# Seven block products back from FF in every other step, eight in the others, and the gate read from the accumulator banks

## The chip, the cores and the metric

The kernel runs on one core of a Trainium2 chip. The time is device microseconds of one execution: 3052.83 us as the median of three runs (3049.15 to 3056.44). The profiled execution took 3051.49 us, of which 3049.7 us is the span from its first to its last instruction. The engines are named as in the profile: PE (matrix products; PEld its weight loads), DVE, ACT and POOL (elementwise work), SP (issues the transfers). PSUM is the memory of eight banks that PE accumulates into; DVE and ACT read it, POOL does not.

## The reference

```python
X = np.fft.rfft(x, axis=1)                       # x: 8 x 3008 x 256
Yr = Xr @ w_r - Xi @ w_i + b_r                   # 256 x 256 weights
Yi = Xr @ w_i + Xi @ w_r + b_i
Yr = np.sign(Yr) * np.maximum(np.abs(Yr) - 0.01, 0.0)     # the same for Yi
y = np.fft.irfft(Yr + 1j * Yi, n=3008, axis=1)   # 24064 tokens of 256
h = y @ w_in                                     # 256 x 2048
g = h * np.clip(h + 3.0, 0.0, 6.0) / 6.0
return g @ w_out                                 # 2048 x 256
```

Nearly all the work is in the last three lines, which are called FF below.

## The kernel before, in words

**FF in steps.** The tokens are cut into 47 chunks of 512. The 2048 hidden features are cut into 4 quarters of 512. A step is one chunk and one quarter, so there are 188 of them (`quads`). Both matrix products of a step are made as a 2 x 2 block product by Winograd's scheme, with seven block products where the plain scheme needs eight. On the way into FF (`up_1` to `up_7`) they are accumulated in two PSUM banks, `px` and `py`: `up_1` starts `px`, ACT copies it into `py` (L966), `up_2` adds to `py`, and so on, until four blocks of h (128 features x 512 tokens each, `hs[i][:, 0..3]`) are read out. Every block product is done as three passes of fp32r matmuls over two halves, since each operand is a high and a low part: six matmuls of 256 columns (L943).

**The gate and the operands for the way back.** Block 0 is gated straight from `py`: ACT makes relu(h + 3) (L972), DVE takes the minimum with 6 and multiplies by h (L973). Blocks 1, 2 and 3 are first brought to SBUF (L990 and L1000 on DVE, L995 on ACT) and gated there in the next step, two blocks at once and then one (L1006 on ACT, L1007 on DVE). Then Winograd's sums of the gated blocks are formed on POOL: T1 and T3 in one subtraction (L1016), T2 (L1038) and nT4 (L1039). Each of b11, b22, b21, T1, T3, T2, nT4 is split into a high part by ACT (`split`, L134) and a low part, the rest, by a subtraction (L135). The subtraction is on DVE for all but b11, where it is on POOL. They go two at a time (1024 columns), b11 alone (512).

**The way back** (`down`): seven block products, accumulated over the four quarters in the banks `z0` to `z3`, with weights that are loaded from DRAM for every step (`load_weights`, L1047, 256 KB for one product). After a chunk's last quarter the four banks are combined and sent out (`finish`, L1075, L1085).

**The order.** Iteration i of the main loop holds `up` of step i, the elementwise work of step i-1 and `down` of step i-2. The code calls their parts in an order that is written out by hand, and into eight slots of an iteration it lays the pieces of the Fourier part of the next sequences (`fill`): that part makes the tokens (`segment`, `stage1`, `middle`, with their own matmuls into the two `side` banks) and, by `prepare`, the seven operands `yb` of the way in, with sums (L913) and low parts on POOL (L135). Engines work through their queues in order, and a scheduler may swap calls that lie close together. The program begins with some 127 us in which the first sequence is transformed and the weights are split; the steps follow.

In the profile L134 and L135 are the two lines of `split`, whatever calls it; the names of the tiles tell which: g (operands of the way back), yb (of the way in), X, z, xs (Fourier part).

Of the kernel before, what the change touches and what calls it, by code (L numbers as in the profile page):

```python
# [25 lines left out]
P = 128  # L26
# [75 lines left out]
def spectral_ffn(ctx: ExitStack, tc: tile.TileContext, x, w_r, w_i, bias, w_in, w_out, f47, f64, g64, g64u, sgn, out):  # L102
# [7 lines left out]
    depth = {"g2": 3, "yb": 7, "wo": 7, "raw": 2, "h": 2, "r": 3, "ot": 2, "bt": 2, "f64": 2}  # L110

    def space(shape, dt, name, tag=None):
        tag = tag or name
        return sb.tile(shape, dt, name=name, tag=tag, bufs=depth.get(tag, 1))
# [57 lines left out]
    wout_d = [dram.tile([7, P, 2, 2, P], F32, name=f"w_out{q}") for q in range(nf // 2)]  # L172
# [22 lines left out]
    class Band:  # L195

        def __init__(self, into, f, tags, home):
            self.into, self.f, self.home = into, f, home
            src = w_in if into else w_out
# [21 lines left out]
        def rest(self):  # L221
# [8 lines left out]
            s = self.sums = self.st.bitcast(F32).rearrange("p (n c) w -> p n (c w)", n=8)[:, :4]  # L230
            for to, p, q, op in (
# [8 lines left out]
        def opened(self):  # L240
            if not hasattr(self, "forms"):
                if self.into:
                    self.forms = [t[:, self.f] for t in win_s]
                else:
                    self.pair = space([P, 7, 2, P], F32R, "wt", self.home)
                    self.forms = [self.pair[:, :, n] for n in range(2)]
            return self.forms

        def upper(self):
            nc.scalar.copy(out=self.opened()[0][:, :3], in_=self.value[:, 1:])  # L250

        def sums_hi(self):
            nc.scalar.copy(out=self.opened()[0][:, 3:], in_=self.sums)

        def sums_lo(self):
            for part, src in ((slice(0, 3), self.value[:, 1:]), (slice(3, 7), self.sums)):
                hi, lo = (t[:, part] for t in self.forms)
                nc.vector.tensor_tensor(out=lo, in0=src, in1=hi.bitcast(F32), op=ALU.subtract)
            if not self.into:
                q, half = divmod(self.f, 2)  # L260
                nc.sync.dma_start(out=wout_d[q][:, :, half].rearrange("m p w c -> p m w c"), in_=self.pair.bitcast(F32))
# [446 lines left out]
    def middle(b):  # L708
# [11 lines left out]
        def s2(g):  # L720
# [16 lines left out]
            xi = space([P, 2, P], F32, "xi")  # L737
# [70 lines left out]
    def segment(b, k):  # L808
# [35 lines left out]
        def odd_part(ps, n):  # L844
            odd = space([P, 2 * R47], F32, "odd", "wo" if begins else "xi")[:, :n]
# [83 lines left out]
    SLOT = {"b11": 0, "b12": 1, "b22": 2, "b21": 3}  # L929
    DOWN = (("b21", 2, "z0", 1), ("b11", 1, "z0", 0), ("b22", 3, "z2", 0), ("T1", 5, "z2", 1))  # L930
    DOWN += (("T3", 7, "z1", 0), ("T2", 6, "z1", 1), ("nT4", 4, "z3", 0))
# [3 lines left out]
    def behind_start(ins, first):  # L935
        tc.add_manual_dep(ins.ins, first.ins.name, after, reason="bank cleared")

    def passes(to, weight, moving, start, stop=True, first=None, later=False):
# [3 lines left out]
        for n, (a, b) in enumerate(todo):  # L942
# [3 lines left out]
            if n == 0:  # L946
                begin_ = ins
                if first is not None:
                    behind_start(ins, first)
        return begin_  # L950
# [17 lines left out]
    def up_2(i):  # L968
        py = keep.pop((i, "y"))
        block(i, 2, py, False)  # L970
        r = space([P, T], F32, "p1")
        nc.scalar.activation(out=r, in_=py, func=AF.Relu, bias=3.0, scale=1.0)  # L972
        nc.vector.scalar_tensor_tensor(out=hs[i][:, 0], in0=r, scalar=6.0, in1=py, op0=ALU.min, op1=ALU.mult)  # L973
# [28 lines left out]
    def gate(i, at):  # L1002

        h = hs[i][:, at]
        r = space([P, *h.shape[1:]], F32, "r")
        nc.scalar.activation(out=r, in_=h, func=AF.Relu, bias=3.0, scale=1.0)  # L1006
        nc.vector.scalar_tensor_tensor(out=h, in0=r, scalar=6.0, in1=h, op0=ALU.min, op1=ALU.mult)  # L1007

    def gate_2(i):
        gate(i, slice(2, 4))  # L1010

    def gate_1(i):
        gate(i, 1)
        h = hs[i]
        t = keep[i, "T13"] = space([P, 2, T], F32, "r")
# [287 lines left out]
```

## Time and profile before

| | before |
|---|---|
| median of 3 runs | 3052.83 us |
| the profiled execution | 3051.49 us, span 3049.7 us |
| busy share of the span | PE 86%, PEld 82%, DVE 84%, ACT 67%, POOL 76% |
| mean granted PE clock | 0.959 of full speed |
| matmuls | 19,887, of which 15,792 in FF |
| loads of the weights of the way back | 1,316 of 256 KB |

A duration in the profile runs from the start to the end of an instruction, so it holds whatever the instruction waited for once it had begun. The ends of matmuls are modelled, and neighbours overlap; the distance between their starts is the pace. "Idle before" is time in which an engine had nothing running, put down to what ended it.

### The profile page before, as it was taken

What the parts mean: (1) busy time and instruction counts of PE and PEld (TensorE: products, weight loads), DVE (VectorE), ACT (ScalarE), POOL (GpSimd) and SP (SyncE); (2) the same over time, 40 slices, a digit from 0 to 9 for tenths busy, and PEclk for the clock granted to TensorE, in tenths of its full rate; (3) what the DMA queues carried; (4) which work ended last, traced back from release to release, by engine and by line L of the source; (5) the groups of instructions that cost most, each with busy time, mean ns of one, the idle gap of its engine ahead of it and who ended that gap; (6) DMA issues with size and microseconds to landing.
All of it is one profiled execution on the core that took longest, in us unless ns stands there. A gap on an engine that the chain in (4) does not pass through costs nothing.

```text
span 3049.7 us, 55092 instructions
## 1 busy us (share of the span) xinstructions
PE 2637.1 (86%) x19887; PEld 2500.2 (82%) x19887; DVE 2570.9 (84%) x3011; ACT 2033.8 (67%) x3480; POOL 2330.0 (76%) x1490
## 2 busy tenths in 40 slices
PE   9688888888888888888898888888798898898888
PEld 6578888878887888888888888888788888888887
DVE  6778888987897889988897888888788998878787
ACT  5566766766666666666666766667576766666665
POOL 3286787887787877788876887788876776788887
PEclk9899999999999999999999999999999999999999
DMA  7765665665655656556565655666556555555554
GB/s 264 245 183 173 199 198 167 195 200 164 183 166 183 187 168 189 175 179 191 166 185 173 184 183 178 183 190 194 165 177 183 174 175 168 172 162 163 153 156 153
DMA packets 343913, 552.66 MB, mean 181 GB/s; under 512 B 37471, under 2 KB 130007, under 8 KB 343639
## 3 DMA queue, kind: packets, MB, share of 16 engines
q1 hardware_dynamic: 343639, 549.14, 58.9%
q8 instruction: 156, 2.56, 0.4%
q14 instruction: 118, 0.97, 0.1%
HBM read 444.66 MB, written 82.31 MB: 173 GB/s over the span
## 4 chain that ended last, share of the span: by engine, by line
POOL 28%; DVE 22%; PE 19%; issue 12%; ACT 11%; DMA 3%; SPq 0%; POOLq 0%; DVEq 0%; ACTq 0%
POOL r L1016 8%; PE z L943 6%; DVE g L135 6%; POOL yb L135 5%; POOL r L1039 4%; DVE h L1007 4%; PE py L943 4%; PE side L141 4%; POOL r L1038 4%; ACT g L134 4%; PE px L943 4%; POOL g L135 3%; DVE tc L767 2%; POOL T L913 2%; DVE ot L1075 1%
## 5 line engine op out<-in xcount | busy, mean ns | idle before, releaser
L943 PE MATMUL z<-g,wo 128*128 128x256 f32 x7896 | 1136.1, 288 | 6.4 <-DVE g L135 2.3
L943 PEld LDWEIGHTS z<-g,wo 128*128 128x128 f32 x7896 | 1043.7, 196 | 16.3 <-DVE g L135 3.2
L135 DVE TENSOR_TENSOR g<-r,g 128x1024 fp32r<-128x1024 f32 x376 | 560.3, 1490 | 155.1 <-ACT g L134 147.8
L134 ACT CAST g<-r 128x1024 fp32r<-128x1024 f32 x376 | 394.4, 1049 | 426.8 <-POOL r L1016 191.4
L943 PE MATMUL px<-yb,w_in_hi 128*128 128x256 f32 x3008 | 581.7, 286 | 1.4 <-POOL yb L135 1.4
L943 PE MATMUL py<-yb,w_in_lo 128*128 128x256 f32 x1128 | 353.6, 313 | 217.2 <-ACT py L966 102.7
L1016 POOL TENSOR_TENSOR r<-h 128x1024 f32<-128x1024 f32 x188 | 487.4, 2592 | 49.3 <-DVE h L1007 46.4
L135 DVE TENSOR_TENSOR g<-h,g 128x1024 fp32r<-128x1024 f32 x188 | 428.6, 2280 | 87.2 <-ACT g L134 86.1
L1007 DVE SCALAR_TENSOR_TENSOR h<-r,h 128x1024 f32<-128x1024 f32 x376 | 486.9, 1302 | 14.1 <-ACT r L1006 12.8
L943 PE MATMUL px<-yb,w_in_lo 128*128 128x256 f32 x1504 | 443.3, 295 | 46.5 <-ACT h L995 31.5
L943 PEld LDWEIGHTS px<-yb,w_in_hi 128*128 128x128 f32 x3008 | 474.6, 194 | 5.1 <-POOL yb L135 1.8
L135 POOL TENSOR_TENSOR g<-h,g 128x512 fp32r<-128x512 f32 x188 | 308.8, 1642 | 180.4 <-ACT g L134 167.5
L943 PEld LDWEIGHTS py<-yb,w_in_lo 128*128 128x128 f32 x1128 | 218.9, 194 | 270.4 <-ACT py L966 123.8
L943 PE MATMUL py<-yb,w_in_hi 128*128 128x256 f32 x2256 | 439.2, 287 | 0.0
L943 PEld LDWEIGHTS py<-yb,w_in_hi 128*128 128x128 f32 x2256 | 358.5, 195 | 1.9 <-issue 0.5
L1039 POOL TENSOR_TENSOR r<-h,r 128x512 f32<-128x512 f32 x188 | 342.4, 1821 | 11.2
L1006 ACT ACTIVATE r<-h 128x1024 f32<-128x1024 f32 x376 | 318.3, 847 | 40.8 <-DVE h L990 36.0
L943 PEld LDWEIGHTS px<-yb,w_in_lo 128*128 128x128 f32 x1504 | 292.7, 195 | 64.2 <-ACT h L995 39.3
L1038 POOL TENSOR_TENSOR r<-h,r 128x512 f32<-128x512 f32 x188 | 327.8, 1744 | 9.7
L134 ACT CAST g<-h 128x512 fp32r<-128x512 f32 x376 | 313.8, 835 | 26.6 <-PE z L943 15.0
L977 ACT COPY u<-px 128x512 f32<-128x512 f32 x376 | 221.2, 588 | 84.1 <-PE px L943 80.4
L135 POOL TENSOR_TENSOR yb<-raw,yb 128x256 fp32r<-128x256 f32 x138 | 160.4, 1163 | 114.0 <-ACT yb L134 113.7
(205 smaller groups left out, 4605.2 us busy)
## 6 DMA issues: line engine op xcount, KB each, us to landing
wo<-w_out SPq DMA_DIRECT2D x1316, 256.0 KB, 3.2
xin<-in_x SPq DMA_DIRECT2D x48, 512.0 KB, 4.3
bt<-scr SPq DMA_DIRECT2D x96, 256.0 KB, 3.3
scr<-pt SPq DMA_DIRECT2D x96, 256.0 KB, 2.9
out<-ot SPq DMA_DIRECT2D x94, 256.0 KB, 3.2
scr<-a SPq DMA_DIRECT2D x96, 240.0 KB, 3.1
qt<-scr SPq DMA_DIRECT2D x96, 240.0 KB, 4.2
zt<-tc SPq DMA_DIRECT2D x336, 64.0 KB, 2.0
```

What stands on the lines that cost most here:

```text
L134: nc.scalar.copy(out=hi, in_=src)
L135: (on or nc.vector).tensor_tensor(out=lo, in0=src, in1=hi.bitcast(F32), op=ALU.subtract)
L141: nc.tensor.matmul(out=ps, lhsT=a, rhs=b, start=start and n == 0, stop=stop and n == len(todo) - 1, skip_group_check=more,)
L767: nc.vector.scalar_tensor_tensor(out=t, in0=t, scalar=LAM, in1=c, op0=ALU.add, op1=ALU.min)
L913: on.tensor_tensor(out=s[:, to], in0=p, in1=q, op=ALU.subtract)
L943: ins = nc.tensor.matmul(out=to, lhsT=a, rhs=b, start=start and n == 0, stop=stop and n == 2, skip_group_check=True)
L977: nc.scalar.copy(out=t, in_=keep[i, "x"])
L1006: nc.scalar.activation(out=r, in_=h, func=AF.Relu, bias=3.0, scale=1.0)
L1007: nc.vector.scalar_tensor_tensor(out=h, in0=r, scalar=6.0, in1=h, op0=ALU.min, op1=ALU.mult)
L1016: nc.gpsimd.tensor_tensor(out=t, in0=h[:, 1:3], in1=h[:, 0:2], op=ALU.subtract)
L1038: nc.gpsimd.tensor_tensor(out=t[:, 0], in0=h[:, 2], in1=t1, op=ALU.subtract)
L1039: nc.gpsimd.tensor_tensor(out=t[:, 1], in0=h[:, 3], in1=t[:, 0], op=ALU.subtract)
```

## The change

There are two kinds of steps in the changed kernel, by quarter: "C", "W", "C", "W". In a W step the way back has the seven products as before. In a C step it has the eight products of the plain scheme: four operands (b11, b12, b21, b22), which are the gated blocks themselves, each used twice, against the four weight blocks, each used twice. Both kinds add into the same four banks; `DOWN` tells which product goes where, and `finish` combines the banks. POOL's three subtractions and the operand pairs (T1, T3) and (T2, nT4) are then made in W steps only; C steps split b12 instead.

The gate is called within the step that makes the block (`gated`): blocks 0, 1 and 3 are read from `py`, `py` and `px`, and block 2 from SBUF. For block 1 the sum with u2 is written back into `py`, and gated from there. ACT no longer copies block 3 out. The low part of b11 is made by DVE and not by POOL. Buffers are renamed: each operand pair has its own (`gA` to `gD`), the gate's intermediate r has the two buffers `p1`, shared with two tiles of the Fourier part, and POOL's sums keep the three of `r`. A weight load is issued when the product that last reads a buffer has been placed.

```diff
-    depth = {"g2": 3, "yb": 7, "wo": 7, "raw": 2, "h": 2, "r": 3, "ot": 2, "bt": 2, "f64": 2}
+    depth = {"yb": 7, "wo": 7, "raw": 2, "h": 2, "r": 3, "ot": 2, "bt": 2, "f64": 2, "p1": 2}
...
+    KINDS = "CWCW"
+    FORMS = ("a21", "a11", "a12", "a22", "S1", "S2", "S3", "S4")
...
-    DOWN = (("b21", 2, "z0", 1), ("b11", 1, "z0", 0), ("b22", 3, "z2", 0), ("T1", 5, "z2", 1))
-    DOWN += (("T3", 7, "z1", 0), ("T2", 6, "z1", 1), ("nT4", 4, "z3", 0))
+    DOWN = {
+        "W": (
+            ("b21", "a12", "z0", 1),
...
+        "C": (
+            ("b21", "a12", "z0", 1),
+            ("b21", "a22", "z3", 0),
+            ("b22", "a12", "z2", 0),
+            ("b22", "a22", "z3", 1),
+            ("b11", "a11", "z0", 1),
...
+    def gated(i, h, to):
+        r = space([P, T], F32, "r", "p1")
+        nc.scalar.activation(out=r, in_=h, func=AF.Relu, bias=3.0, scale=1.0)
+        nc.vector.scalar_tensor_tensor(out=hs[i][:, to], in0=r, scalar=6.0, in1=h, op0=ALU.min, op1=ALU.mult)
...
     def up_5(i):
...
-        nc.vector.tensor_tensor(out=hs[i][:, 2], in0=py, in1=keep.pop((i, "u3")), op=ALU.add)
+        h = hs[i][:, 2]
+        nc.vector.tensor_tensor(out=h, in0=py, in1=keep.pop((i, "u3")), op=ALU.add)
+        gated(i, h, 2)
 
     def up_4(i):
         px = keep.pop((i, "x"))
         block(i, 4, px, False)
-        nc.scalar.copy(out=hs[i][:, 3], in_=px)
+        gated(i, px, 3)
 
     def up_3(i):
         py = keep.pop((i, "y"))
         block(i, 3, py, False)
-        nc.vector.tensor_tensor(out=hs[i][:, 1], in0=py, in1=keep.pop((i, "u2")), op=ALU.add)
...
+        nc.vector.tensor_tensor(out=py, in0=py, in1=keep.pop((i, "u2")), op=ALU.add)
+        gated(i, py, 1)
+
+    def sums_1(i):
+        if kind(i) == "W":
+            h = hs[i]
+            t = keep[i, "T13"] = space([P, 2, T], F32, "r")
+            nc.gpsimd.tensor_tensor(out=t, in0=h[:, 1:3], in1=h[:, 0:2], op=ALU.subtract)
...
-        operands(i, ("b11",), hs[i][:, 0:1], "g1", nc.gpsimd)
...
+    def operands_A(i):
+        operands(i, ("b11",), hs[i][:, 0:1], "gA")
+
+    def operands_C(i):
+        if kind(i) == "W":
+            operands(i, ("T1", "T3"), keep.pop((i, "T13")), "gC")
+
+    def operands_D(i):
         h = hs.pop(i)
...
+        if kind(i) == "W":
+            operands(i, ("T2", "nT4"), keep.pop((i, "T24")), "gD")
+        else:
+            operands(i, ("b12",), h[:, 1:2], "gD")
```

**What moves on POOL.** Both pieces are the end of POOL's work on the 23rd chunk's operands yb; r is a tile of Winograd sums, g the low part of b11. Before:

```order
L1016 TENSOR_TENSOR r<-h 128x1024
L135 TENSOR_TENSOR g<-h,g 128x512
L135 TENSOR_TENSOR yb<-raw,yb 128x256
L1038 TENSOR_TENSOR r<-h,r 128x512
L135 TENSOR_TENSOR yb<-T,yb 128x256
L1039 TENSOR_TENSOR r<-h,r 128x512
L135 TENSOR_TENSOR yb<-T,yb 128x256 x3
L135 TENSOR_TENSOR g<-h,g 128x512
L135 TENSOR_TENSOR yb<-raw,yb 128x256
L1016 TENSOR_TENSOR r<-h 128x1024
L1038 TENSOR_TENSOR r<-h,r 128x512
L1039 TENSOR_TENSOR r<-h,r 128x512
```

And in the changed kernel:

```order
L1051 TENSOR_TENSOR r<-h 128x1024
L1057 TENSOR_TENSOR r<-h,r 128x512
L1058 TENSOR_TENSOR r<-h,r 128x512
L139 TENSOR_TENSOR yb<-raw,yb 128x256 x2
L139 TENSOR_TENSOR yb<-T,yb 128x256 x4
L139 TENSOR_TENSOR yb<-raw,yb 128x256
L1051 TENSOR_TENSOR r<-h 128x1024
L1057 TENSOR_TENSOR r<-h,r 128x512
L1058 TENSOR_TENSOR r<-h,r 128x512
```

The two sets of sums of the second piece are two steps apart, and no g is left on POOL.

**What moves on DVE.** Both pieces begin with the gate of block 0 of step 92 and go on to that of step 93 (g, X and z are low parts, u a kept copy of `px`). Before:

```order
L973 SCALAR_TENSOR_TENSOR h<-p_18904,py 128x512
L135 TENSOR_TENSOR g<-h,g 128x1024
L990 TENSOR_TENSOR h<-py,u_18940 128x512
L135 TENSOR_TENSOR g<-r,g 128x1024
L135 TENSOR_TENSOR z<-zt,z 128x512
L1000 TENSOR_TENSOR h<-py,u_18913 128x512
L1007 SCALAR_TENSOR_TENSOR h<-r,h 128x1024
L135 TENSOR_TENSOR g<-r,g 128x1024
L1007 SCALAR_TENSOR_TENSOR h<-r,h 128x512
L973 SCALAR_TENSOR_TENSOR h<-p_19072,py 128x512
```

And in the changed kernel, where the low parts are first those of a C step's operands, and the last one is of a W step's:

```order
L1003 SCALAR_TENSOR_TENSOR h<-r,py 128x512
L139 TENSOR_TENSOR g<-h,g 128x512
L1033 TENSOR_TENSOR h<-py,u_18733 128x512
L1003 SCALAR_TENSOR_TENSOR h<-r,h 128x512
L139 TENSOR_TENSOR g<-h,g 128x512
L139 TENSOR_TENSOR z<-zt,z 128x512
L1003 SCALAR_TENSOR_TENSOR h<-r,px 128x512
L1044 TENSOR_TENSOR py<-py,u_18705 128x512
L1003 SCALAR_TENSOR_TENSOR h<-r,py 128x512
L139 TENSOR_TENSOR g<-r,g 128x1024
L1003 SCALAR_TENSOR_TENSOR h<-r,py 128x512
```

Four gates of 512 columns stand where one of 512 from `py`, one of 1024 and one of 512 stood, three of them with px or py as an input, and the last gate on py stands two instructions behind the sum that it reads.

**What moves on ACT.** The rows around the copy of `px` into `py` that opens step 92 (L966 before, L1010 after). Before:

```order
L1006 ACTIVATE r<-h 128x1024
L134 CAST g<-r 128x1024
L770 ACTIVATE tc<-tc,sgn 128x256
L738 COPY xi<-side 128x256
L134 CAST X<-side 128x2x256
L966 COPY py<-px 128x512
L134 CAST yb<-raw 128x256
L1006 ACTIVATE r<-h 128x512
L134 CAST g<-h 128x512
```

And in the changed kernel:

```order
L1002 ACTIVATE r<-px 128x512
L791 ACTIVATE tc<-tc,sgn 128x256
L1002 ACTIVATE r<-py 128x512
L759 COPY xi<-side 128x256
L138 CAST X<-side 128x2x256
L138 CAST g<-r 128x1024
L1010 COPY py<-px 128x512
```

The relu of block 1, read from py, now stands ahead of the copy that opens the next step, where before it stood behind it.

## Rows read from the trace of the kernel before

**Rows 1.** The page: busy time, share of the span, instructions.

```profile
PE 2637.1 (86%) x19887; PEld 2500.2 (82%) x19887; DVE 2570.9 (84%) x3011; ACT 2033.8 (67%) x3480; POOL 2330.0 (76%) x1490
```

**Rows 2.** Groups by form: count, busy us, mean ns, idle before and its releasers.

```profile
L1016 POOL TENSOR_TENSOR r<-h 128x1024 f32<-128x1024 f32 x188 | 487.4, 2592 | 49.3 <-DVE h L1007 46.4 <-DMA scr<-a 2.9
...
L1039 POOL TENSOR_TENSOR r<-h,r 128x512 f32<-128x512 f32 x188 | 342.4, 1821 | 11.2
L1038 POOL TENSOR_TENSOR r<-h,r 128x512 f32<-128x512 f32 x188 | 327.8, 1744 | 9.7
L135 POOL TENSOR_TENSOR g<-h,g 128x512 fp32r<-128x512 f32 x188 | 308.8, 1642 | 180.4 <-ACT g L134 167.5 <-issue 12.0 <-POOL xs L135 0.3
...
L1007 DVE SCALAR_TENSOR_TENSOR h<-r,h 128x512 f32<-128x512 f32 x188 | 217.7, 1158 | 5.1 <-ACT r L1006 4.2
```

**Rows 3.** Single lines: duration ns min/median/max, first and last start.

```profile
L1016 POOL TENSOR_TENSOR r<-h x188: 2334/2402/3457, 150.7 to 3033.6; 128x1024 f32<-128x1024 f32 x188
...
L1038 POOL TENSOR_TENSOR r<-h,r x188: 1255/1625/2342, 153.2 to 3037.0; 128x512 f32<-128x512 f32 x188
...
L1039 POOL TENSOR_TENSOR r<-h,r x188: 1256/2134/2468, 154.6 to 3038.3; 128x512 f32<-128x512 f32 x188
...
L135 DVE TENSOR_TENSOR g<-r,g x376: 1207/1316/2358, 154.2 to 3041.6; 128x1024 fp32r<-128x1024 f32 x188
...
L135 POOL TENSOR_TENSOR g<-h,g x188: 1256/1628/2292, 131.4 to 3031.6; 128x512 fp32r<-128x512 f32 x188
...
L135 DVE TENSOR_TENSOR g<-h,g x188: 1209/2285/6072, 149.0 to 3033.4; 128x1024 fp32r<-128x1024 f32 x188
...
L1007 DVE SCALAR_TENSOR_TENSOR h<-r,h x376: 674/1219/2325, 145.7 to 3031.7; 128x1024 f32<-128x1024 f32 x188
...
L973 DVE SCALAR_TENSOR_TENSOR h<-p,py x188: 669/675/691, 130.0 to 3021.8; 128x512 f32<-128x512 f32 x188
```

**Rows 4.** Timeline, POOL's and DVE's instructions from 1524.0: start, us, engine.

```profile
1524.03 1.29 POOL L135 TENSOR_TENSOR g<-h,g 128x512 fp32r<-128x512 f32 x1
...
1524.56 1.84 DVE L135 TENSOR_TENSOR g<-h,g 128x1024 fp32r<-128x1024 f32 x1 [1.10 <-ACT g L134]
...
1525.28 3.39 POOL L1016 TENSOR_TENSOR r<-h 128x1024 f32<-128x1024 f32 x1
...
1526.33 2.88 DVE L135 TENSOR_TENSOR z<-zt,z 128x512 fp32r<-128x512 f32 x1
...
1529.14 0.68 DVE L990 TENSOR_TENSOR h<-py,u 128x512 f32<-128x512 f32 x1
```

**Rows 5.** Waits of PE: us in total, times, longest.

```profile
PE py L943 <- ACT py L966: 102.7, 86, 4.9
PE py L943 <- DVE h L990: 86.0, 82, 5.9
PE side L141 <- DVE raw L865: 56.4, 19, 6.9
```

**Rows 6.** Waits of ACT, the same columns.

```profile
ACT g L134 <- POOL r L1016: 191.4, 82, 4.8
...
ACT g L134 <- POOL r L1039: 143.0, 80, 4.6
```

**Rows 7.** Busy time of the steps' stretch: us, PE, PEld, DVE, ACT, POOL; clock, DMA share, GB/s.

```profile
127.00:3044.00 2917.00, 2531.31 (x19282) 2423.54 (x19283) 2479.71 (x2840) 1964.35 (x3330) 2296.24 (x1435) 0.96 0.59 178
```

**Rows 8.** The chain that ended last, around 1515 us: start, us, what.

```profile
1515.33 1.65 PE py L943 x6
...
1519.88 1.43 PE z L943 x12
```

**Rows 9.** Groups by form, ACT's.

```profile
L1006 ACT ACTIVATE r<-h 128x512 f32<-128x512 f32 x188 | 118.6, 631 | 1.4 <-DVE h L1000 1.4
...
L972 ACT ACTIVATE p<-py 128x512 f32<-128x512 f32 x188 | 112.4, 598 | 18.5 <-PE py L943 15.9
L995 ACT COPY h<-px 128x512 f32<-128x512 f32 x188 | 109.8, 584 | 30.1 <-PE px L943 29.6
```

More of the change, by code (lines that the diff above doesn't have):

```diff
@@ L198, in __init__ @@
             self.into, self.f, self.home = into, f, home
+            self.plain = not into and KINDS[f // 2] == "C"
             src = w_in if into else w_out
@@ L946, in passes @@
             if n == 0:
-                begin_ = ins
+                begun_ = ins
                 if first is not None:
-                    behind_start(ins, first)
-        return begin_
+                    tc.add_manual_dep(ins.ins, first.ins.name, after, reason="bank cleared")
+        return begun_
     def block(i, n, to, start):
@@ L999, in up_3 @@
         block(i, 3, py, False)
-        nc.vector.tensor_tensor(out=hs[i][:, 1], in0=py, in1=keep.pop((i, "u2")), op=ALU.add)
[L1002 to L1015, printed above, removed]
-        nc.gpsimd.tensor_tensor(out=t, in0=h[:, 1:3], in1=h[:, 0:2], op=ALU.subtract)
@@ new lines, in operands_A @@
+    def operands_A(i):
[4 more added lines that the diff above has]
+    def operands_D(i):
+        h = hs.pop(i)
+        if kind(i) == "W":
+            operands(i, ("T2", "nT4"), keep.pop((i, "T24")), "gD")
+        else:
+            operands(i, ("b12",), h[:, 1:2], "gD")
+    loads = []
+    for j in range(len(quads)):
+        names = [n for _, n, _, _ in DOWN[kind(j)]]
+        loads += [(j, n) for n in dict.fromkeys(names)]
@@ L1049, in down, with load_weights @@
+    used = {}
+    loaded_ = [0]
+    def load_weights():
+        while loaded_[0] < len(loads):
+            n = loaded_[0]
+            if n >= depth["wo"] and not used.get(loads[n - depth["wo"]]):
+                return
+            j, name = loads[n]
+            t = wo[j, name] = space([P, 2, 2, P], F32R, "wo")
+            nc.sync.dma_start(out=t.bitcast(F32), in_=wout_d[quads[j][1]][FORMS.index(name)])
+            loaded_[0] += 1
     def down(j, at):
         c, q = quads[j]
-        name, n, z, side = DOWN[at]
@@ L1052, in down @@
-        w = wo.pop((j, at))
-        g = forms.pop((j, name))
-        begins = q == 0 and z not in zs
-        if begins:
-            zs[z] = bank(z), None
-        to, first = zs[z]
+        todo = DOWN[kind(j)]
+        if at >= len(todo):
+            return
+        name, n, z, side = todo[at]
+        w, g = wo[j, n], forms[j, name]
+        if z not in zs:
+            zs[z] = [bank(z), None, set()]
+        to, first, halves = zs[z]
         for ab in range(2):
@@ L1062, in down @@
                 tuple(half(t, ab) for t in g),
-                start=begins and ab == 0,
+                start=first is None,
                 stop=q == nq - 1 and ab == 1,
-                first=first if q == 0 and ab == 0 else None,
+                first=first if side not in halves else None,
                 later=True,
             )
-            if begins and ab == 0:
-                zs[z] = to, ins
-        load_weights(j + 1, at)
+            if first is None:
+                zs[z][1] = first = ins
+            halves.add(side)
+        if n not in [m for _, m, _, _ in todo[at + 1 :]]:
+            used[j, n] = True
+            del wo[j, n]
+            load_weights()
+        if name not in [m for m, _, _, _ in todo[at + 1 :]]:
+            del forms[j, name]
     sixth = 1.0 / 6.0
@@ L1128, in later @@
             if n == len(todo_bands) + 2:
-                for at in range(7):
-                    load_weights(0, at)
+                load_weights()
         yield
@@ L1251, in spectral_ffn @@
         down_(6)
[L1252 removed]
         filled(6)
+        down_(7)
+        now(operands_D, i - 1)
         filled(7)
```

126 lines of the change are left out of this document (71 added, 55 removed).

## The prediction

> **What bounds the kernel now.** I read the page first. By busy shares no engine is full: PE 86%, DVE 84%, POOL 76% [rows 1]. The first question for such a profile is whether busy time is work. For DVE and POOL it isn't: the same instruction takes very different times. A split of 1024 columns takes 1207 ns at its shortest and 2285 in the median on one line, a 512-column subtraction on POOL 1255 to 2468 [rows 3]. The gate of block 0, which reads PSUM, never leaves 669 to 691 ns, while the same operation with both inputs in SBUF has a mean of 1158 [rows 2, 3].
>
> The timeline says what stretches them [rows 4]. POOL holds its subtraction to 1525.32. The DVE split that began at 1524.56 ends at 1526.40, 1.1 us after that, about its bare 1.2. POOL's next, begun at 1525.28, ends 2.3 us after the split, its bare 2334 ns. The DVE subtraction on z ends 0.5 us after POOL's. So a DVE instruction with two SBUF inputs and a POOL instruction run one after the other, never together, and whoever waits counts as busy. DVE instructions with an input in PSUM are not held up.
>
> The two engines thus share one resource, and it can be budgeted with shortest durations (an estimate). POOL: 188 x (2334 + 1255 + 1256 + 1256) = 1147 us for its four FF instructions. They are busy 1466 us [rows 2], so the ratio is 0.78; the other 864 us of POOL at about 0.7 give 590. Sum 1740. DVE with two SBUF inputs: 564 splits x 1207 = 681, gates 188 x (1207 + 674) = 354, some 150 for the Fourier part: 1180. Together 2920 of 3050 us, 96%. This shared access is the bound, and the busy shares hide it.
>
> PE suffers from it at second hand. It is idle for 2917 - 2531 = 386 us of the steps' stretch [rows 7]. The long waits are for `py` from ACT (103), for `py` from L990 (86) and for the side bank from L865 (56) [rows 5]. In the first case ACT itself stands behind POOL's sums, for 191 and 143 us [rows 6]; in the second and third DVE is late. After a wait PE is also slow: six matmuls in 1.65 us, then twelve in 1.43 [rows 8], 0.275 and 0.119 us each, the two levels of its clock.
>
> **The change part by part.**
>
> PE: 94 C steps get one product more, 94 x 6 = 564 matmuls. At the full pace of 0.119 us that is +67 us, on the path if PE sets the pace.
>
> POOL: the three sums go in 94 steps, 94 x (2334 + 1255 + 1256) = 455 us of bare time, and b11's subtraction in all 188, 236 us [rows 3].
>
> DVE with two SBUF inputs, bare, for two neighbouring steps. Before: 2 x (3 x 1207 + 1207 + 674) = 11.0 us. After, a W step: 3 x 1207 + 674 (b11) + 674 (gate of block 2) = 4.97; a C step: 1207 + 674 (b11) + 674 (b12) + 674 = 3.23; together 8.2. That is -2.8 x 94 = -264 us. The shared access falls by 455 + 236 + 264 = 955 us to about 1965, 64% of the span. It can no longer be the bound of the whole, though a W step's share is still 4.97 + 4.85 (POOL's sums) + 3.9 for the rest, 13.7 us, against 7.1 in a C step.
>
> DVE in all keeps its work: the three gates and two sums that touch PSUM take about 0.68 each [rows 3], and what C steps save in splits goes into b11 and into four gates instead of three. The sum of block 1 writes PSUM, for which DVE has no row. From below it costs the 0.67 of the PSUM readers; from above I take the 1158 of the slowed SBUF form [rows 2], 0.5 us x 188 = 90 us of DVE time. I take 0.68, because the nearest row has an operand in PSUM and 512 columns.
>
> Here the Trainium skill speaks against the change: "VectorE: DVE Perf Modes", section "Rules for kernel authors", says that elementwise work on a matmul's output either accepts the PSUM rate or should copy to SBUF first if several operations follow, as the kernel before does for blocks 1 to 3. Here the copy to SBUF lengthened the gate, 1158 ns on the mean against the 675 of block 0's, so the trace bears that rule out only for a lone engine. By it the sum would lose the relief of two gates, some 90 us on DVE.
>
> ACT: a relu takes 598 from PSUM and 631 from SBUF, and the copy of block 3 (584) goes [rows 9]. C steps drop a 1024 cast and halve another. It is relieved by about 1.2 us a step and bounds nothing.
>
> Transfers: 7 + 4 weight loads for two steps instead of 14. Seven buffers hold a C step's four blocks and three of the next W step's, so loads stay ahead; I cost this at nothing, and a late load would show as PE waiting for wo.
>
> Waits added: `py` is given back only after sum, relu and gate of block 1, where the sum was enough; that is 0.60 + 0.68 = 1.28 us longer, plus hand-offs. `px` is held by relu and gate, 1.28, where a copy took 0.58. The copy L1010 waits for the gate on ACT, and behind it stand the next relu and casts, for which DVE and then PE wait. The cover: between `up_3` and the next `up_2` PE has 24 to 30 matmuls of other work, 2.9 to 3.6 us, and some Fourier matmuls; the bare chain of sum, relu, gate and copy is 0.68 + 0.60 + 0.68 + 0.58 = 2.5. So it is just hidden when DVE and ACT are at hand, and costs up to 1.28 x 188 = 241 us where they are not. I take 50 us, a fifth, since the queues that now fill DVE and ACT are those that stand behind POOL.
>
> **The sum.** The steps' stretch has 19,282 matmuls. At 0.119 us they are 2295, and with the longer ones of 512 columns about 2350. What is left of PE's busy time, 2531 - 2350 = 181, is slow clock and tails of matmuls before a wait; it goes with the waits. Idle before: 386. Of it some 280 stand in the waits that POOL and the shared access cause (103, 86, 56, and smaller ones for the side bank); I let a quarter of them, 70, remain, because W steps are still full. The other 106 (px, block 0's gate) fall to 80 with ACT's relief. With 50 new ones: 200. The slow part scales, 181 x 200 / 386 = 94. So 133 us ahead of and behind the stretch + 2350 + 67 + 200 + 94 = 2844; against the profiled execution's 3051.5 (1.3 below the median) I forecast 2845 us, its own range 2780 to 2895.
>
> **Rivals.**
> 1. The relief goes further: waits of 110 us, as DVE and ACT keep ahead in C steps and carry the lead into W steps. 2550 + 110 + 52 = 2712, to 2780. For it: the share of 64%. Against it: a W step's 13.7 us of shared access beside its iteration's some 13.1 of PE work.
> 2. Half the relief: only C steps lose their waits, and the accumulator banks cost 90. Waits 280 and slow part 131: 2961, 2895 to 3040. For it: a pipeline whose queues are in order passes a late DVE on to every bank. Against it: two of PE's three long waits are POOL's doing.
> 3. Slower: the gate in `py` closes the loop. From 0.9 us a step of new wait at `up_2`, 170 us with its slow clock, nothing is gained; at the full 1.28 us the waits are 106 + 70 + 241 = 417, the slow part 196, and the time 2550 + 613 = 3163. For it: `py` has already the longest waits [rows 5]. Against it: 0.4 to 1.1 us of cover over the bare chain.
> 4. PE was the bound all along, its waits stay, and the added products come on top: 2550 + 386 + 181 = 3117. Against it: PE's waits have named causes, and most of them are removed. The Trainium skill, "Perfetto Trace Analysis", section "Identifying the Most-Contended Engine", would have PE judged by its busy weight loads, here 82% [rows 1], nearly DVE's share, which speaks for this rival; the 386 us in which PE stood idle beside that share speak against it.
>
> **How the numbers follow.** Chances: forecast 0.45, rival 1 0.16, rival 2 0.25, no change 0.03, rival 3 0.08, rival 4 0.03. Faster by over 0.2%, about what a measurement of this kernel can tell from no change: 0.86; within: 0.03; slower: 0.11. The range takes in the forecast's, most of rival 2 and the upper half of rival 1, and leaves out those of the slower side: 2715 to 3010 us.
>
> **What would show it.** Right: POOL's busy share near 45%; DVE splits of g near 1.2 to 1.4 us on the mean; PE's busy share above 90%; ACT's waits for L1051 and L1058 under half of 334 us; PE's wait for L990's successor (L1033) well below 86. Wrong: splits as long as before with POOL idle, so that something else stretches them; or PE's waits for the copy L1010 above 200 us, which is rival 3; or waits for the gate at `px` above 100; or the same idle time on PE with new names, rival 2.

## The result and the profile after

The changed kernel took 2809.78 us (2805.51 to 2814.11, four runs) against 3050.99 of the kernel before on the same chip: a ratio of 0.9208 with an interval of 0.9186 to 0.923, or 241 us less. The forecast was 2845, with a range of 2715 to 3010. The profiled execution took 2805.51 us.

The page after answers to [rows 1]:

```profile
PE 2625.2 (94%) x20451; PEld 2503.2 (89%) x20451; DVE 2185.5 (78%) x3336; ACT 1814.6 (65%) x3382; POOL 1291.5 (46%) x1004
```

PE has 564 matmuls more and is busy 12 us less. POOL's busy time fell by 1039 us.

The groups by form after (count, busy us, mean ns, idle before and its releasers) answer to [rows 2] and [rows 3]:

```profile
L139 DVE TENSOR_TENSOR g<-h,g 128x1024 fp32r<-128x1024 f32 x188 | 274.7, 1461 | 50.7 <-ACT g L138 50.0
L139 DVE TENSOR_TENSOR g<-r,g 128x1024 fp32r<-128x1024 f32 x188 | 265.0, 1409 | 251.4 <-ACT g L138 229.7 <-PE z L982 21.5
...
L139 DVE TENSOR_TENSOR g<-h,g 128x512 fp32r<-128x512 f32 x282 | 241.0, 855 | 30.7 <-ACT g L138 29.2 <-PE py L982 0.3
L1051 POOL TENSOR_TENSOR r<-h 128x1024 f32<-128x1024 f32 x94 | 226.5, 2409 | 327.1 <-DVE h L1003 327.1
...
L1058 POOL TENSOR_TENSOR r<-h,r 128x512 f32<-128x512 f32 x94 | 195.4, 2079 | 7.1
...
L1003 DVE SCALAR_TENSOR_TENSOR h<-r,h 128x512 f32<-128x512 f32 x188 | 142.8, 760 | 33.0 <-ACT r L1002 29.8
...
L1044 DVE TENSOR_TENSOR py<-py,u 128x512 f32<-128x512 f32 x188 | 129.6, 689 | 0.1
```

All of these are means. The split of b22 and b21 takes 1461 ns where it took 2280, the 512-column gate that still reads SBUF 760 where it took 1158, and POOL's large sum 2409, near its bare 2334. POOL now stands idle ahead of that sum for 327 us: it waits for work. POOL's last sum of a W step (L1058, nT4) has not become shorter: 2079 ns, where L1039 took 1821. The two engines still hold each other up within W steps.

The waits of PE after (us in total, times, longest), for [rows 5]:

```profile
PE px L982 <- ACT u L1019: 76.1, 68, 4.6
PE py L982 <- DVE h L1003: 22.7, 27, 1.8
PE px L982 <- DVE h L1003: 12.4, 24, 1.4
PE py L982 <- ACT py L1010: 10.4, 15, 3.2
...
PE side L145 <- POOL xs L139: 5.8, 2, 4.9
PE py L982 <- DVE h L1033: 5.4, 9, 1.2
...
PE side L145 <- DVE raw L886: 3.0, 9, 0.5
```

The three long waits of before have nearly gone: 103 became 10.4 (`py` from ACT's copy), 86 became 5.4 (the sum of block 2), 56 became 3.0 (side bank). A new one leads, `px` for ACT's copies u, 76 us. The timeline shows where it comes from (start, us, engine; only the rows of ACT, POOL and PE that belong together):

```profile
1407.69 2.39 POOL L1051 TENSOR_TENSOR r<-h 128x1024 f32<-128x1024 f32 x1 [7.72 <-DVE h L1003]
1407.70 0.57 ACT L1010 COPY py<-px 128x512 f32<-128x512 f32 x1 [0.81 <-DVE h L1003]
...
1410.12 1.05 ACT L138 CAST g<-r 128x1024 fp32r<-128x1024 f32 x1 [1.85 <-POOL r L1051]
...
1411.08 0.58 ACT L1002 ACTIVATE r<-py 128x512 f32<-128x512 f32 x1
...
1411.56 0.57 ACT L1019 COPY u<-px 128x512 f32<-128x512 f32 x1
...
1412.19 0.39 PE L982 MATMUL px<-yb,w_in_lo 128*128 128x256 f32 x1 [1.19 <-ACT u L1019]
```

POOL's sum T1, T3 can begin only when block 1 is gated, the last of the four. ACT's cast of that sum stands at the head of ACT's queue, and behind it stand the relu of the next step's block 0 and the copy u2, until which PE cannot go on in `px`. In the code the call for this cast stands behind both copies of the step; the scheduler has moved it ahead of them. ACT waits 168 us in total for L1051:

```profile
ACT r L1002 <- DVE py L1044: 170.8, 131, 2.5
ACT g L138 <- POOL r L1051: 168.4, 93, 5.2
```

The stretch of the steps answers to [rows 7] (us, PE, PEld, DVE, ACT, POOL; clock, DMA share, GB/s):

```profile
127.00:2798.00 2671.00, 2517.01 (x19841) 2424.84 (x19841) 2093.99 (x3165) 1745.94 (x3235) 1264.53 (x961) 0.99 0.54 167
```

PE's idle time in it is 2671 - 2517 = 154 us, 386 before; the granted clock is 0.99, 0.96 before.

### The profile page after: what moved, and what is told of

Read it like the earlier page. It is cut to its first block, busy times and chain, and to the rows that moved or that the text cites. A ratio compares the mean times of both kernels' runs of the same rounds, so it can differ in the third digit from the quotient of the medians.

```text
span 2803.7 us, 55242 instructions
## 1 busy us (share of the span) xinstructions
PE 2625.2 (94%) x20451; PEld 2503.2 (89%) x20451; DVE 2185.5 (78%) x3336; ACT 1814.6 (65%) x3382; POOL 1291.5 (46%) x1004
## 4 chain that ended last, share of the span: by engine, by line
PE 39%; DVE 19%; issue 12%; POOL 12%; ACT 11%; DMA 3%; SPq 0%; ACTq 0%; DVEq 0%; POOLq 0%
PE z L982 15%; PE px L982 8%; PE py L982 7%; POOL r L1051 7%; DVE h L1003 6%; PE side L145 6%; DVE g L139 6%; ACT g L138 4%; ACT r L1002 2%; POOL T L934 2%; DMA xin<-in_x 2%; PE side L857 1%; DVE py L1044 1%; DVE h L1033 1%; PE side L747 1%
## 5 line engine op out<-in xcount | busy, mean ns | idle before, releaser
L139 DVE TENSOR_TENSOR g<-h,g 128x512 fp32r<-128x512 f32 (+1 forms) x470 | 514.5, 1097 | 81.4 <-ACT g L138 79.2
L139 DVE TENSOR_TENSOR g<-r,g 128x1024 fp32r<-128x1024 f32 x188 | 265.0, 1409 | 251.4 <-ACT g L138 229.7
L138 ACT CAST g<-h 128x512 fp32r<-128x512 f32 (+1 forms) x470 | 373.3, 794 | 125.0 <-PE z L982 121.5
L1051 POOL TENSOR_TENSOR r<-h 128x1024 f32<-128x1024 f32 x94 | 226.5, 2409 | 327.1 <-DVE h L1003 327.1
L1002 ACT ACTIVATE r<-py 128x512 f32<-128x512 f32 x376 | 223.8, 595 | 184.5 <-DVE py L1044 170.8
L138 ACT CAST g<-r 128x1024 fp32r<-128x1024 f32 x188 | 197.7, 1051 | 215.5 <-POOL r L1051 168.4
L1003 DVE SCALAR_TENSOR_TENSOR h<-r,py 128x512 f32<-128x512 f32 x376 | 255.9, 681 | 69.9 <-ACT r L1002 65.2
L1058 POOL TENSOR_TENSOR r<-h,r 128x512 f32<-128x512 f32 x94 | 195.4, 2079 | 7.1
L934 POOL TENSOR_TENSOR T<-raw,T 128x256 f32<-128x256 f32 x92 | 97.1, 1055 | 212.1 <-DVE raw L886 107.6
L139 POOL TENSOR_TENSOR yb<-T,yb 128x256 fp32r<-128x256 f32 x184 | 154.0, 850 | 83.0 <-ACT yb L138 78.6
```

What stands on the lines that cost most here:

```text
L138: nc.scalar.copy(out=hi, in_=src)
L139: (on or nc.vector).tensor_tensor(out=lo, in0=src, in1=hi.bitcast(F32), op=ALU.subtract)
L934: on.tensor_tensor(out=s[:, to], in0=p, in1=q, op=ALU.subtract)
L1003: nc.vector.scalar_tensor_tensor(out=hs[i][:, to], in0=r, scalar=6.0, in1=h, op0=ALU.min, op1=ALU.mult)
L1051: nc.gpsimd.tensor_tensor(out=t, in0=h[:, 1:3], in1=h[:, 0:2], op=ALU.subtract)
L1058: nc.gpsimd.tensor_tensor(out=t[:, 1], in0=h[:, 3], in1=t[:, 0], op=ALU.subtract)
```

## The experiments

All times are medians, with ratios to the kernel before on the same chip; the brackets hold the 95% interval. Theory A is the prediction's: POOL's instructions and DVE's with two SBUF inputs exclude each other, and this shared access bound the kernel before.

The prediction read the exclusion from one stretch of some 5 us [rows 4]. In the trace of the kernel before it can be counted over all the steps, by asking of each instruction whether the other engine was running when it began. Of DVE's 1226 instructions with two SBUF inputs, 338 began while POOL ran nothing, and none of these took more than 21 ns over the shortest of its line and shape. The other 888 began beside a running POOL instruction and took 701 ns more than the shortest, on the mean. It is the same the other way: L1039 on POOL took 1256 to 1304 ns when no such DVE instruction was running at its start (61 times), and 2080 on the mean when one was (127 times). The gate that reads `py` (L973) stayed within 669 to 691 ns in both cases. One of the two, a POOL instruction or a DVE instruction with two SBUF inputs, was running for 2712 of the stretch's 2917 us, 93%, beside the 96% of the prediction's budget.

### One part alone, in the kernel before

```diff
-        operands(i, ("b11",), hs[i][:, 0:1], "g1", nc.gpsimd)
+        operands(i, ("b11",), hs[i][:, 0:1], "g1")
```

> The kernel before with one edit: the low part of b11 (188 subtractions of 512 columns) goes from POOL to DVE. Theory A (POOL instructions and DVE instructions with two SBUF inputs exclude each other, and that shared access is the bound of the kernel before): POOL's 1256 ns become DVE's 674 ns on the same access, 188 x 0.58 = 109 us less, so 2890 to 2950 us against 3051, although DVE, the fuller engine, gets 127 us more to do. Rival B (each engine is bound by its own work, DVE first with 84%): 3051 to 3180 us, slower.

2962.1 us, 0.9709 (0.9685 to 0.9734). The fuller engine was given 188 instructions more, and the kernel became 88 us faster. That is against rival B. It is 0.8 of the 109 us of shared access, and 2962 lies 12 us outside the 2890 to 2950 that A expected. By itself the run doesn't tell A from a POOL whose own queue is late; the count above does. The page of this run, and one of PE's waits:

```profile
PE 2606.4 (88%) x19887; PEld 2471.9 (83%) x19887; DVE 2673.0 (90%) x3199; ACT 2031.9 (69%) x3480; POOL 2084.0 (70%) x1302
```

```profile
PE py L943 <- DVE h L973: 64.7, 55, 3.0
```

The wait for block 0's gate was 27.5 us before. A fuller DVE comes to that gate later, and this took back a part of the gain.

### Two sums of POOL left out, in the kernel before

```diff
-        t = keep[i, "T24"] = space([P, 2, T], F32, "r")
-        nc.gpsimd.tensor_tensor(out=t[:, 0], in0=h[:, 2], in1=t1, op=ALU.subtract)
-        nc.gpsimd.tensor_tensor(out=t[:, 1], in0=h[:, 3], in1=t[:, 0], op=ALU.subtract)
+        keep[i, "T24"] = h[:, 2:4]
```

> The kernel before without POOL's two 512-column sums of a step (L1038, L1039): the operands T2 and nT4 are split from blocks 2 and 3 instead, so their values are not Winograd's. PE, ACT and DVE keep every instruction. Theory A (POOL and DVE's two-SBUF instructions exclude each other): 472 us less on the shared access, 2920 to 2450; the DVE splits of b22 and b21, of which nothing is changed, fall from a mean of 2280 ns to 1300 to 1800; time 2750 to 2900 us. Rival B (DVE's long splits are its own, or the memory's): their mean stays above 2100 ns.

(The kernel leaves out Winograd's T2 and nT4, so its results are not those of the reference.) 2831.09 us, 0.9279 (0.9265 to 0.9293). DVE has the 3011 instructions of before [rows 1]:

```profile
PE 2570.6 (91%) x19887; PEld 2451.2 (87%) x19887; DVE 2420.9 (86%) x3011; ACT 2026.5 (72%) x3480; POOL 1643.4 (58%) x1114
```

The group of DVE's large splits by form in the same run:

```profile
L135 DVE TENSOR_TENSOR g<-h,g 128x1024 fp32r<-128x1024 f32 x376 | 654.6, 1741 | 81.9 <-ACT g L134 80.6
```

DVE's 3011 instructions take 150 us less, and POOL does 472 us less of bare work (376 sums of 1255 ns). The group of splits that read h now holds T2 and nT4 too, so its 1741 ns is the mean of two kinds. They can be told apart, since the one of b22 and b21 always comes first in a step: it takes 2128 ns, T2's and nT4's 1353. So the test that was named for A failed on its line: 2280 fell to 2128, not to 1300 to 1800. That split mostly begins beside what is left on POOL, the sum L1016 (75 of 188) or the low part of b11 (44). The split of T1 and T3 had stood beside the two sums, and it went from 1578 to 1309. In this run, too, the 291 splits of 1024 columns that began with POOL idle took their bare time, at most 1228 ns. So A's exclusion holds, and only which instructions the two sums had stretched was guessed wrong. The access was now in use for 2297 of the stretch's 2697 us, 85%, and no longer full.

### The other part alone: new gates, seven products in every step

```diff
-    KINDS = "CWCW"
+    KINDS = "WWWW"
...
-            onto(half(ot, 1), half(z, 1), half(ot, 0))
+            nc.scalar.copy(out=half(ot, 1), in_=half(ot, 0))
...
-        now(operands_C, i - 1)
...
         down_(6)
+        now(operands_C, i - 1)
```

The call moves because with two W steps in succession the buffer of T1 is read until the last product. ACT copies in place of one sum because in W steps no product goes into the second half of `z3`.

> The changed kernel with seven products in every step (KINDS WWWW; the combination at the end of a chunk without the half bank that no W step writes). It has the gates from PSUM and b11 on DVE, but POOL's sums in all 188 steps. Theory A: shared access 2920 - 236 (b11 off POOL) - 188 x (1881 - 674 - 674 ns) = 2585 us, 85 to 90% of the span, PE 67 us below the changed kernel: 2830 to 2920 us, so both parts of the change carry the gain. Rival C (the gain is the C steps' alone): 3000 or more. Rival D (the gates and b11 are the whole gain, eight products only cost PE time): 2740, 67 below the changed kernel.

3118.71 us, 1.0215 (1.0194 to 1.0237): slower than the kernel before. All that A expected here fails, and the time lies where rival C had it; but C's reason, that the gain is the C steps' alone, doesn't fit with the 88 us that b11's move gave by itself. The page and PE's waits:

```profile
PE 2688.5 (86%) x19887; PEld 2515.8 (81%) x19887; DVE 2631.1 (84%) x3387; ACT 1961.4 (63%) x3527; POOL 1905.3 (61%) x1302
```

```profile
PE py L982 <- DVE h L1003: 156.0, 103, 4.8
PE px L982 <- ACT u L1019: 71.5, 72, 4.0
PE px L982 <- DVE h L1003: 56.1, 65, 2.8
PE z L982 <- ACT g L138: 31.3, 35, 2.8
PE z L982 <- DVE g L139: 18.2, 34, 0.8
PE py L982 <- ACT py L1010: 11.2, 13, 4.4
PE z L982 <- DMA wo<-w_out: 9.7, 10, 1.8
```

By the prediction's budget the shared access is 2585 of 3118 us, 83%, and no longer full; counted in the trace it was in use for 2422 of the stretch's 2985 us, 81%. PE waits 212 us for gates, L1003 at `py` and `px`. The 156 at `py` are for block 0's gate: `up_5` starts the bank anew behind it. One of these waits in the timeline (start, us, engine):

```profile
1536.98 0.59 ACT L1002 ACTIVATE r<-py 128x512 f32<-128x512 f32 x1
...
1537.76 3.98 DVE L139 TENSOR_TENSOR g<-h,g 128x512 fp32r<-128x512 f32 x2
...
1541.67 0.68 DVE L1003 SCALAR_TENSOR_TENSOR h<-r,py 128x512 f32<-128x512 f32 x1
1542.40 0.38 PE L982 MATMUL py<-yb,w_in_lo 128*128 128x256 f32 x1 [2.58 <-DVE h L1003]
```

The relu is done at 1537.57, and the gate begins 4.1 us later, behind two low parts that hold no bank. Over the 103 waits the gate began 2.8 us after its relu on the mean, 289 us in all, and DVE ran low parts g for 198 of them. So a gate that holds a bank stands in DVE's queue behind work that holds none. But block 0's gate was read from PSUM before as well. Of the gates that the change moved, block 3's has 56 us (ACT's copy of that block had 12 in the run with old gates and b11 on DVE), and the hold of `py` by block 1, which is rival 3's mechanism, has no more than the 11 us at `py` behind the copy L1010. Another 59 us are waits at `z` for operands and weights.

### Is it ACT's order?

In the changed kernel, the cast of T1 and T3 is put behind the copy u3 on ACT:

```diff
-        nc.scalar.copy(out=t, in_=keep[i, "x"])
+        lastcopy[0] = nc.scalar.copy(out=t, in_=keep[i, "x"])
...
-        split(t[:, 0], t[:, 1], src)
+        cast = nc.scalar.copy(out=t[:, 0], in_=src)
+        if behind_ is not None:
+            tc.add_manual_dep(cast.ins, behind_.ins.name, after, reason="behind the copy")
+        nc.vector.tensor_tensor(out=t[:, 1], in0=src, in1=t[:, 0].bitcast(F32), op=ALU.subtract)
...
-            operands(i, ("T1", "T3"), keep.pop((i, "T13")), "gC")
+            operands(i, ("T1", "T3"), keep.pop((i, "T13")), "gC", lastcopy[0])
```

> The changed kernel with one edit: on ACT the high part of T1 and T3 stands behind the copy u3 of the next step instead of ahead of the relu of block 0 and the copies u2 and u3. In the changed kernel ACT waits there for POOL's sum L1051 (168 us), and PE's longest wait is px for the copies (76 us, with the weight load 97). If that wait is on the path: PE's wait for the copies falls under 30 us, and with its slow clock 50 to 80 us go: 2730 to 2760. If it only moves (to the operands T1, T3 or to py): 2795 to 2820.

2724.22 us, 0.8928 (0.8911 to 0.8945): 86 us less than the changed kernel, and more than expected, from one instruction's place. PE's waits:

```profile
PE px L982 <- DVE h L1003: 23.9, 40, 1.7
PE py L982 <- ACT py L1010: 15.7, 26, 3.8
...
PE px L982 <- ACT u L1021: 6.4, 7, 2.7
```

76 us of waits for the copies became 6.4, so that wait was on the path. In the stretch of the steps PE's idle time fell by 65 us and its busy time by 20. The same edit with seven products in every step:

> Seven products in every step with the new gates, and the cast of T1 and T3 behind the copy u3. If the 157 us by which the new gates lose in W steps are ACT's order (casts that stand ahead of copies and relus): under 3020. If they are DVE's lateness (the gates in px and py stand behind full splits, PE waits for L1003 at py and px, 212 us): 3050 to 3130.

3144.3 us, 1.0303 (1.0288 to 1.0319): 26 us slower than without the edit, and 14 above the range expected for gates that DVE delays. PE's waits for gates are the same, and those for the copies are longer:

```profile
PE py L982 <- DVE h L1003: 154.3, 107, 4.8
PE px L982 <- ACT u L1021: 92.9, 55, 4.0
PE px L982 <- DVE h L1003: 58.2, 66, 4.5
```

So in W steps alone that cast is not what costs. The 154 and 58 us for gates that come late from DVE are left. Why the edit made the run slower is not shown.

### The fourth corner: C steps with the gates of before

```diff
-        gated(i, px, 3)
+        nc.scalar.copy(out=hs[i][:, 3], in_=px)
...
         now(up_1, i)
+        now(gate_2, i - 1)
         down_(0)
+        filled(0)
+        now(gate_1, i - 1)
         now(sums_1, i - 1)
-        filled(0)
```

(`gate_1` and `gate_2` are those of the kernel before; blocks 1 and 2 are only summed in `up_3` and `up_5`.)

> The changed kernel with the gates of before: blocks 1, 2, 3 go to SBUF and are gated in the next step, 1024 and 512 columns at once; C steps, b11 on DVE, buffers and order are those of the changed kernel. With the run before (old gates, b11 on DVE, only W steps: 2962) and the one with new gates and only W steps (3119) it makes a square of four. If parts add up, C steps bring 311 us and the old gates 157: 2650 us. If the new gates cost only where DVE is full, as in W steps, and are nearly free here: 2770 to 2830. If the gates from PSUM are a gain in C steps, by the shared access (227 us less with them): 2850 to 2900.

2826.15 us, 0.9264 (0.9243 to 0.9285), within the 2770 to 2830 expected if the new gates are nearly free here. With the runs above, and with b11's low part on DVE in all four:

| | seven in every step | every other step with eight |
|---|---|---|
| old gates | 2962 | 2826 |
| new gates | 3119 | 2810 |

In the right column the new gates give 16 us (the two ratios, 0.9264 and 0.9208, have intervals that don't meet), and there only the gates differ, with their place in the order and their buffers for r. In the left column the lower corner is 157 us slower. But the left upper corner has the order and buffers of the kernel before, so these 157 us hold those too, and they are not shown to be the price of the gates: most of PE's waits in the lower corner are for block 0's gate, for the copies u and at `z`, as above.

### What the hold of `py` costs

```diff
-        nc.vector.tensor_tensor(out=py, in0=py, in1=keep.pop((i, "u2")), op=ALU.add)
-        gated(i, py, 1)
+        h = hs[i][:, 1]
+        nc.vector.tensor_tensor(out=h, in0=py, in1=keep.pop((i, "u2")), op=ALU.add)
+        gated(i, h, 1)
```

> The changed kernel with one edit: the sum of block 1 goes to SBUF (hs) and is gated there, as block 2 is, so py comes free after the sum, 1.28 us earlier, and DVE gets 188 more instructions with two SBUF inputs (127 us on the shared access, 64 to 68%). Theory A: the gate's mean rises from 681 to 720 to 900 ns, py's waits on PE (41 us) shrink, time 2795 to 2825 against 2808, no clear difference. Rival 3 of the prediction (the hold of py is what is left on the path): 2740 to 2780.

2793.7 us, 0.9159 (0.9136 to 0.9181), 16 us less than the changed kernel. Together with the cast behind the copies:

> Both edits that were faster alone: block 1 gated from SBUF (2794) and the cast behind the copies (2724) in the changed kernel. If they take different waits: 2705 to 2718. If PE, 96% busy, is the bound: 2715 to 2735, no difference from the cast alone.

2695.4 us, 0.8838 (0.8824 to 0.8853), 29 us less than the cast alone and 10 below the lowest that was expected. The edit was worth 16 and 29 us, and the expectation of no clear difference in the first run was wrong. The waits don't show that this is the hold: PE's wait at `py` for the copy L1010 went from 10.4 to 12.1 us in the first run and from 15.7 to 12.4 in the second, and what fell was PE's busy time (2625.2 to 2609.0, and 2605.0 to 2581.4). What shortened that is open.

### b11 back on POOL, in the changed kernel

```diff
-        operands(i, ("b11",), hs[i][:, 0:1], "gA")
+        operands(i, ("b11",), hs[i][:, 0:1], "gA", nc.gpsimd)
```

> The changed kernel with one edit: the low part of b11 goes back to POOL (188 x 1256 ns on the shared access in place of 674 ns, 109 us more, 64 to 68% of the span; DVE 127 us less). In the kernel before the same step the other way gained 88 us. If the shared access is no longer the bound: 2800 to 2830 us against 2809, no gain and little loss. If DVE's own load is what is left: 2740 to 2790. If the shared access still binds: 2880 or more.

2832.93 us, 0.9279 (0.9264 to 0.9294): 23 us lost, where the same step the other way gave 88 in the kernel before; it is 3 us over the range expected if the access is no longer the bound. The shared access has stopped being the bound, but it is still felt. Counted in the trace of the changed kernel, it was in use for 1856 of the stretch's 2671 us, 69%.

### How many C steps

Both on the fastest so far, block 1 from SBUF and the cast behind the copies:

```diff
-    KINDS = "CWCW"
+    KINDS = "CCCW"
```

> The fastest so far (2695: block 1 from SBUF, cast behind the copies) with quarters C, C, C, W: 47 steps more with eight products, 282 matmuls x 0.119 = 34 us of PE, and 47 x 6.6 = 310 us less on the shared access. PE waits 85 us there and loses some 60 to its slow clock. If the waits are mostly the W steps': half of them go, 2650 to 2690. If PE is simply full: 2715 to 2735. If the relief goes on as from four W steps to two (over 100 us for 47 steps): below 2620.

2659.72 us, 0.8711 (0.8698 to 0.8724), as expected if the waits are mostly the W steps'.

> The same with quarters C, W, W, W: 34 us of PE less, 310 us more on the shared access, and W steps in succession, in which DVE has no lighter step to catch up. If PE is the bound wherever a C step lies between: 2660 to 2700. If the loss is by steps that follow a W step (half of the way to 3144, which all W steps took): 2870 to 2960.

(`CWWW`, with the call of `operands_C` moved as above.) 2854.23 us, 0.9346 (0.9332 to 0.936), a little better than expected; the waits for gates are back:

```profile
PE px L982 <- DVE h L1003: 73.1, 78, 3.0
PE py L982 <- DVE h L1003: 64.0, 57, 2.6
```

Last, C steps alone:

```diff
-    KINDS = "CWCW"
+    KINDS = "CCCC"
...
+        if at == 7:
+            z = zs.pop("z3")[0]
+            ot1 = keep.pop("ot1")
+            nc.scalar.mul(out=half(ot1, 1), in_=half(z, 1), mul=sixth)
             nc.sync.dma_start(out=out[P:, c * T : (c + 1) * T], in_=ot1)
```

(The other three results of a chunk are copied out in the same way at 4, 5 and 6.)

> The fastest so far (2660, quarters C, C, C, W) with four C quarters: no sums on POOL at all, 282 matmuls more (34 us at the full pace), and the four results of a chunk copied out by ACT in place of eight sums on DVE. PE is idle for 45 us of the stretch of the run before and loses some 40 to its slow clock. If PE is full, the products cost what they take, less a part of the waits: 2665 to 2695, slower than three C quarters, so the best mix has a W quarter. If the waits that the last W quarter causes weigh more than its seventh product saves: below 2655.

2659.41 us, 0.8706 (0.8691 to 0.872), the same as with three C steps of four, and between the two cases expected (2665 or more, below 2655). The pages of these two runs, three of four and then all:

```profile
PE 2593.5 (97%) x20733; PEld 2510.8 (94%) x20733; DVE 2031.6 (76%) x3287; ACT 1762.3 (66%) x3333; POOL 961.3 (36%) x855
```

```profile
PE 2609.8 (98%) x21015; PEld 2536.3 (95%) x21015; DVE 1783.9 (67%) x2854; ACT 1743.4 (66%) x3425; POOL 665.5 (25%) x714
```

PE is busy 97 and 98% of the span. In the stretch of the steps its idle time fell from 45 to 29 us with the last W quarter, and its busy time rose by 15, although the 270 matmuls more of that stretch would be 32 us at 0.119: what the last W steps save in products they cost in waits and slow clock. The series with four, three, two, one and no W quarter (3144, 2854, 2695, 2660, 2659 us) falls steeply and then lies flat, which fits with a bound that passes from DVE and POOL to PE. (The first of the five still has block 1 gated from `py`, and the last another combination at a chunk's end.)

## Why the prediction was right, point by point

**The bound before: right, with a limit.** That a full resource was hidden behind three engines at 76 to 86% was shown from three sides: the access is in use for 93% of the steps' stretch, and instructions that found it free took their bare time; work moved onto the fuller engine made the kernel faster; and DVE's busy time fell when POOL had less to do. The budget's 96% is a little high against that 93%. (One of its terms is a slip: 864 us at 0.7 are 605, not 590.) The limit is in what the budget can say. It said that a kernel with 83% of shared access has room; the run with seven products in every step had 83% by it and was slower than the one with 96%. The access is one bound; the order in which a busy DVE gets to the instructions that hold PE's banks is another.

**The sum: PE's terms right, the terms of the waits wrong in both directions.** The 133 us outside the stretch were met: 2805.5 - 2671 = 134. PE's busy time in the stretch was 2517 us against 2350 + 67 + 94 = 2511; taken at the forecast's pace of 0.119 us a matmul (2417 us), this leaves a slow part of 100 against 94. The waits were 154 against 200. Their parts were not those of the prediction. The three long waits, which stood behind POOL and the shared access and of which I let 70 remain with the smaller ones, shrank to under 20 (10, 5 and 3 us). The 80 for others are some 59. The 50 for new ones were 76, and not at `py`, where I had them, but at `px`, from ACT's cast that stands ahead of the copies. Counted as I had counted the waits of before, these 76 stand behind POOL too, since ACT waits there for POOL's sum: 95 against 70. It is no longer POOL's load, though, for POOL stands idle ahead of that sum; it is the order. That the sum comes within 35 us of the measured time is in part luck: terms that were too high stand beside one that was too low. I had read the rows of ACT in which that cast stands ahead of L1010, and wrote what stands behind L1010; I didn't follow the cast's own wait to the copies of `px`. At 86 us, its measured price, that was worth three to five times what block 1 from SBUF gave.

**The added hold of `py`: too large, and not seen where I had it.** I took 50 us, between nothing and 241, as a wait at `up_2` behind the copy L1010. That wait was 10.4 us in all. Taking the hold out gave 16 and 29 us, in PE's busy time and not in that wait.

**The gates: the step that was wrong.** Both the 264 us of relief on the shared access, 227 of them by the gates, and the sentence that the queues which fill DVE and ACT "are those that stand behind POOL", made the gates from PSUM worth having by themselves. Where little else differs they give 16 us, in a kernel in which every other step leaves DVE time. With seven products in every step, new gates, order and buffers together lose 157 us to the corner with the old ones; what the prediction had left out is that DVE's queue is late by its own work too, and not only behind POOL: at 84% busy, block 0's gate stood behind low parts, for which PE waited 156 us. Read through the square, the 241 us are b11's move (88), the C steps with order and buffers (136) and the gates (16); in another order of the steps the C steps would have 309.

**Rivals.** Rival 1 came nearest in its reason: DVE and ACT do keep ahead in C steps, and 2724 us were to be had with one instruction moved. Rival 2 had waits of 280 us; they were 154. Rival 3 has the time of the runs without C steps, 3119 and 3144 against its 3163, but that is chance: its wait, at `up_2` behind the copy L1010, was 11 us there, and not 241. Rival 4 is refuted: PE took 67 us more of products and still the kernel became 241 us faster. From three C steps of four on PE is nearly full, 97%.

**What I had named as signs.** POOL at 45% (46), PE above 90% (94), L1033's wait well below 86 (5.4), L1010's under 200 (10) all came. The splits' means of 1409 and 1461 ns are just above the 1.2 to 1.4 us I had named. ACT's waits for POOL's sums, 171 us (168 of them for L1051), are just over the half of 334 that I had set, and that miss was the trace of the cast at the head of ACT's queue.

**What stays open.** How much of the 157 us in W steps alone is the gates', and how much the order's and the buffers', was not shown. A run with seven products, the order of the changed kernel and the old gates would tell, and so would one with DVE's gates moved ahead of its splits; neither was made. Open, too, are why the cast behind the copies made that kernel slower, and what shortened PE's busy time when block 1 was gated from SBUF.

## What to carry to other kernels

Where two engines' instructions lengthen each other, add up their shortest durations on what they share before believing any busy share, and move work by that sum, even onto the fuller engine. Then check the sum against the trace: the time in which one or the other runs, and whether an instruction that finds the access free takes its bare time. A bank that is read in place is held until the reading engine's queue comes to it; here, with DVE 84% busy, PE waited 156 us for one gate that stood behind splits. After such a change look at what stands at the head of each in-order queue: one cast that waited for POOL's sum cost 86 us.

## What the runs showed of the hardware

- A DVE instruction with two SBUF inputs and a POOL instruction wait for each other, whichever comes second: in the kernel before, the 338 of DVE that began with POOL idle took at most 21 ns over the shortest of their line and shape, the 888 that began beside a POOL instruction 701 ns more on the mean. Instructions of DVE with an input in PSUM were not held up (L973, 669 to 691 ns).
- DVE writes PSUM at the rate at which it reads it: the sum back into `py` (L1044) took 681 to 700 ns for 512 columns, 689 in the mean, beside 684 for the sum that writes SBUF (L1033). I had bounded it between 670 and 1158.
- Reading r from SBUF and h from PSUM, the gate stayed at 681 ns in the mean in the changed kernel, as before (679); with both from SBUF it was 760 there, with POOL at 46%, and 782 in the run of 2695 us, with POOL at 47%.
- PE's granted clock rose as its waits went: 0.96 before, 0.99 after, 1.00 over the steps of the last run. In that run 21,015 matmuls, 1128 more than before, took 27 us less busy time in all (2609.8 against 2637.1).
